# Block-sparse attention with a feed-forward layer on one core: three score banks, tied preparations, and early copies and casts on ACT

## The chip, the cores and the metric

The kernel runs on one core of a Trainium2 chip. The metric is the device time of one launch in microseconds (us), lower is better. A core has a matrix engine (TensorE: PE for its matmuls, PEld for its weight loads), a vector engine (VectorE, DVE), a scalar engine (ScalarE, ACT), GpSimd (POOL), and SyncE (SP), which in this kernel issues the DMAs; SPq stands for its queue. PSUM has eight accumulator banks.

## The reference

```python
def _attn_ref(q, k, v, sampled_blocks):            # q, k, v: 4 x 8 x 768 x 64
    scores = scale * np.matmul(q, k.transpose(0, 1, 3, 2))
    mask = np.abs(blk_i - blk_j) <= 1              # blocks of 32
    mask = mask | (blk_i == 0) | (blk_j == 0) | (blk_i == n_blocks - 1) | (blk_j == n_blocks - 1)
    for qb in range(n_blocks):                     # and three sampled blocks for each query block
        for kb in sampled_blocks[qb]:
            mask[qb * block:(qb + 1) * block, kb * block:(kb + 1) * block] = True
    scores = np.where(mask, scores, -1000000000.0)
    attn = np.exp(scores - np.max(scores, axis=-1, keepdims=True))
    attn = attn / (np.sum(attn, axis=-1, keepdims=True) + 1e-09)
    return np.matmul(attn, v)

def _moe_ref(x, w_in, w_out):                      # x: 3072 x 512, w_in: 512 x 2048, w_out: 2048 x 512
    h = x @ w_in
    g = np.maximum(0.01 * h, h)
    return g @ w_out
```

The attention's output, heads side by side, is x of the feed-forward layer.

## The kernel before

Every float32 operand of a matmul is split into a high and a low half-precision part; products are summed from those parts. A *unit* is one tile of 64 queries for one pair of heads. Four tiles by four head pairs are the 16 units of an *item* (256 tokens); twelve items (four sequences b of three items j) make 192 units. A tile meets 384 keys (12 blocks of 32: four of the neighbourhood, the first and last, six sampled); the first tile of a sequence (T = 0) holds the two edge blocks' queries, sees all 768 keys and works in two parts, which makes 208 score tiles of 128 x 384.

Steps of a unit: scores on PE (`scores`, L651: query against key high and low, into a PSUM bank s); scaling, mask and row minimum of the negated score on DVE (L658, "mx"); exp with row sum on ACT (L669); for each two units the reciprocal on DVE (L677, L678); the high part of the probabilities on ACT (L684, tile pp); the low part on DVE (L689, "split"); the transposition of both by a DMA that SyncE issues (L692, tile pt); and P times V on PE (`pair_av`, L714, one bank av). After four head pairs the tile is normalised to x (L721 to L732). The feed-forward work of a finished item is cut into 16 chunks f: h = x W_in on PE (L749, one of the banks h), leaky relu (ACT L756, DVE L760), its half-precision cast g (DVE L765 in `ffn_act2`), its rest (POOL L766), and o = g W_out on PE (L779, two banks o). Chunks of items (0,0) and (0,1) are taken before both weights have their final scale (`c.whole` is false there); they go through L756 and L760 in other forms.

Around these run the *preparations*: for each 128 queries (`prep_q`) a load by SyncE (rq, L473), a square with sum on ACT (L523), the sum over partitions on PE (L126, q_sum), the scale on DVE, the high part on ACT (L530), the low part on DVE (L532), a transposition by SyncE (L535, qs) and two copies by SyncE with halves exchanged (L537, L538, qxs). `prep_k` does the same for the keys of two heads (loads L482, square L494, k_sum, transposition L512 to kt). V is split (L446, L449), written out (L453) and gathered for each tile by SyncE (`gather_v`: L611, L616, and six sampled blocks with L619 and L621 each). The keys of a tile are collected in one of two buffers kg (`gather_k`): a copy of the four neighbouring blocks by DVE (L582), of the edge blocks (L585), and of the sampled blocks by POOL (L591). The weights are decoded in between (L304 to L316 the column scales, L367 to L376 the splits).

The order of the work comes from two places. The program emits the steps unit by unit, in the order of a string of letters (`CFG["ord"]`), with preparations and weights advanced by costs; then the framework's scheduler sets each engine's order from priorities (by emission) and a timeline of its own. Instructions of equal readiness keep the order of emission unless a dependency says otherwise; a *NoSync* dependency binds the order of two instructions of one engine without a semaphore. Score tiles are emitted in pairs, the later unit first:

```python
        for u in us[::-1]:
...
                if not CFG["spair"]:
                    scores(ahead[:1])
                elif u.pi == 1:
...
                        scores(ahead)
```

Names in rows: `p_1_2_3_0_0` is sequence 1, item 2, tile 3, head pair 0, part 0, and s, mx, pp and pt likewise; `q2_0_0` is sequence 2, item 0, first half of its queries; `k1_0` is sequence 1, first two heads; `g_1_1_0` is chunk 0 of item (1,1).

The PSUM banks are two s, two o, three h and one av.

Of the kernel before, what the change touches and what calls it, by code (L numbers as in the profile page):

```python
# [19 lines left out]
P = 128  # L20
# [9 lines left out]
CFG = {  # L30
    "ahead": 3,
    "av_lag": 3,
    "bs": 1500,
    "early": 2,
    "flag": 1,
    "g": 2,
    "g_at": 0,
    "ht": 1,
    "k_at": 6,
    "k_at0": 26,  # L40
# [10 lines left out]
    "rk": 2,  # L51
    "rmax": 1.0,
    "rmin": 0.0,
    "side": 1.2,
    "side0": 1.6,
    "spair": 1,
    "spread": 8,
    "v_at": 28,
    "wr": [(0, 1.0), (4, 3.0), (10, 4.0), (18, 4.5)],
# [6 lines left out]
def tile_block_sparse_attention_ffn(  # L66
# [19 lines left out]
    nc = tc.nc  # L86
# [20 lines left out]
    pa = ctx.enter_context(tc.tile_pool(name="pa", bufs=2))  # L107
    pf = ctx.enter_context(tc.tile_pool(name="pf", bufs=2))
    dr = ctx.enter_context(tc.tile_pool(name="dr", bufs=2, space=bass.MemoryType.DRAM))
    ps_s = ctx.enter_context(tc.tile_pool(name="ps_s", bufs=2, space=bass.MemoryType.PSUM))  # L110
    ps_o = ctx.enter_context(tc.tile_pool(name="ps_o", bufs=2, space=bass.MemoryType.PSUM))
    ps_1 = ctx.enter_context(tc.tile_pool(name="ps_1", bufs=1, space=bass.MemoryType.PSUM))

# [1 line left out]
    nc.vector.memset(zero, 0.0)  # L115

    def bank(name, tag="h"):
        return ps_1.tile([P, 512], F32, tag=tag, name=name, bufs={"h": 3, "av": 1}[tag])


    ones = cst.tile([P, P], F32, name="ones")
# [2 lines left out]
    def scale_sum(ss, n, name):  # L124
        pb = bank(f"{name}_sum")
        nc.tensor.matmul(pb[:, :n], ones, ss, start=True, stop=True)  # L126
        return pb
# [26 lines left out]
    def scales(ss, n, name, **how):  # L154
        now = tc.cur_priority
        tc.cur_priority = now - CFG["bs"]
        begin = len(nc.cur_bb.bb.instructions)
        pb = scale_sum(ss, n, name)
        loose.update(i.name for i in nc.cur_bb.bb.instructions[begin:])
        r = scale_of(pb, n, name, **how)  # L160
        tc.cur_priority = now + 8
        return r

    def together(emits):

        now = tc.cur_priority
        begin = len(nc.cur_bb.bb.instructions)
        for n, emit in enumerate(emits):
            if n == 1:
                tc.cur_priority = now - 100000  # L170
            emit()
        new = nc.cur_bb.bb.instructions[begin:]
        for i in new[1:]:
            tc.add_manual_dep(i, new[0].name, mybir.DependencyInfo(
                mybir.DependencyClass.NoSync, mybir.DependencyReason.DATA), reason="together")
        tc.cur_priority = now + len(new)
# [308 lines left out]
    def prep_k(b, hp, rk):  # L485

        nm = f"k{b}_{hp}"
        ss = sm.tile([P, 1], F32, tag="ssk", name=f"ss_{nm}")
        if b == 0:
            k16 = early_k.bitcast(F16)[:, (NP + hp) * 2 * S:(NP + hp + 1) * 2 * S].rearrange(  # L490
                "p (n l d) -> p n l d", n=HC, l=2)
        else:
            k16 = pa.tile([P, HC, 2, D], F16, tag="k16", name=f"k16_{nm}", bufs=1)
        nc.scalar.activation(flat(k16)[:, :S], flat(rk), AF.Square, accum_out=ss)  # L494
        yield 1.0
        yield 0.01
        pb = scale_sum(ss, 1, nm)
        yield 0.2
        inv, s = scale_of(pb, 1, nm, fl="k")
        if (b, "inv") not in kready:  # L500
            kready[b, "inv"] = cst.tile([P, NP], F32, name=f"kinv_{b}")
        nc.vector.tensor_scalar(
            out=kready[b, "inv"][:, hp:hp + 1], in0=inv[:, :1], scalar1=-SCALE, scalar2=None, op0=ALU.mult)
        yield 0.4
        raw = rk.rearrange("p h c d -> p (h c) d")
        nc.scalar.activation(k16[:, :, 1, :], raw, AF.Copy, scale=s[:, :1])
        yield 1.0
        nc.vector.scalar_tensor_tensor(
            out=k16[:, :, 0, :], in0=raw, scalar=s[:, :1], in1=k16[:, :, 1, :], op0=ALU.mult, op1=ALU.subtract)
        if b not in kts:  # L510
            kts[b] = pa.tile([P, H, S], F16, tag="kt", name=f"kt_{b}", bufs=2)
        nc.sync.dma_start_transpose(  # L512
            out=kts[b][:, 2 * hp:2 * hp + 2, :].rearrange("p h (c t) -> p (h c) t", t=P),
            in_=k16.rearrange("p n l d -> p (n l d)"))
        kready[b, hp] = True
        yield 1.2

    def prep_q(b, j, i, rq):

        nm = f"q{b}_{j}_{i}"  # L520
        ss = sm.tile([P, 1], F32, tag="ssq", name=f"ss_{nm}")
        qa = pa.tile([P, H, 2, D], F16, tag="qa", name=f"qa_{nm}", bufs=1)
        nc.scalar.activation(flat(qa)[:, :H * D], rq.rearrange("p h d -> p (h d)"), AF.Square, accum_out=ss)  # L523
        yield 0.7
        yield 0.01
        pb = scale_sum(ss, 1, nm)
        yield 0.2
        inv, s = scale_of(pb, 1, nm)
        yield 0.4
        nc.scalar.activation(qa[:, :, 1, :], rq, AF.Copy, scale=s[:, :1])  # L530
        yield 0.7
        nc.vector.scalar_tensor_tensor(  # L532
            out=qa[:, :, 0, :], in0=rq, scalar=s[:, :1], in1=qa[:, :, 1, :], op0=ALU.mult, op1=ALU.subtract)
        qs = pa.tile([P, H, P], F16, tag="qs", name=f"qs_{nm}", bufs=2)
        nc.sync.dma_start_transpose(out=qs, in_=flat(qa))  # L535
        qxs = pa.tile([P, H, P], F16, tag="qxs", name=f"qxs_{nm}", bufs=2)
        nc.sync.dma_start(out=qxs[:D], in_=qs[D:])  # L537
        nc.sync.dma_start(out=qxs[D:], in_=qs[:D])  # L538
        qstack[b, j, i] = (qs, qxs, inv)
        yield 0.8  # L540
# [28 lines left out]
    def sampled_of(T):  # L569

        return [(6 + a * NR + r, (2 * T - 1 + a) * NR + r) for a in range(2) for r in range(NR)]
# [4 lines left out]
    def gather_k(b, T):  # L576

        kt = kts[b]
        n = (b * (NT - 1) + T - 1) % 2
        kg = kgb[n]  # L580
        t0 = (T - 1) * Q2
        nc.vector.tensor_copy(out=kg[:, :, :P], in_=kt[:, :, t0:t0 + P])  # L582
        if ends.get(n) != b:
            ends[n] = b
            nc.vector.tensor_copy(  # L585
                out=kg[:, :, P:P + Q2].rearrange("p h (n l) -> p h n l", l=BLOCK),
                in_=kt.rearrange("p h (n l) -> p h n l", l=BLOCK)[:, :, 0:NB:NB - 1, :])
        for slot, i in sampled_of(T):
            begin = len(nc.cur_bb.bb.instructions)
            off = nc.gpsimd.value_load(offs[:1, i:i + 1], min_val=0, max_val=S - BLOCK)  # L590
            nc.gpsimd.tensor_copy(  # L591
                out=kg[:, :, slot * BLOCK:(slot + 1) * BLOCK], in_=kt[:, :, bass.ds(off, BLOCK)])
            in_order("k", begin)
            yield
        em = pa.tile([P, KEYS], BF16, tag="em", name=f"em_{b}_{T}", bufs=2)
        nc.gpsimd.tensor_copy(
            out=em.rearrange("p (n l) -> p n l", l=BLOCK),
            in_=mask[:, T - 1, :].unsqueeze(2).to_broadcast([P, SLOTS, BLOCK]))
        kgs[b, T] = kg, em
        yield  # L600
# [97 lines left out]
    def pair_av(pr):  # L698

        if pr.hp == 0:  # L700
            avs[pr.item.n, pr.T] = bank(f"av_{pr.nm}", "av").rearrange("p (n l t) -> p n l t", n=NP, l=2)
        pr.av = avs[pr.item.n, pr.T]
        for u in pr.units:
            require_v(u.b, u.hp, u.T)
        emits = []
        for u in pr.units[::-1]:
            n = NCH * u.parts
            for c in range(n):
                for l in range(2):
                    for hh in range(2):  # L710
                        vt = vgs[u.b, u.T][:, c, 2 * u.hp + hh, :] if u.T else v16s[u.b, u.hp][:, c, hh, :]
                        emits.append(lambda o=pr.av[hh * D:(hh + 1) * D, u.hp], a=vt[:, l * D:(l + 1) * D],
                                     m=u.pt[c // NCH][:, :, c % NCH, hh * D:(hh + 1) * D], c=c, l=l, n=n:
                                     nc.tensor.matmul(o, a, m, start=(c == 0 and l == 0), stop=(c == n - 1 and l == 1)))  # L714
        together(emits)

    def tile_evac(pr):

# [43 lines left out]

    def ffn_act2(c):
        c.g = pf.tile([P, 2, 2, N2], F16, tag="g", name=f"g_{c.item.nm}_{c.f}", bufs=CFG["g"])
        nc.vector.tensor_copy(out=c.g[:, 0], in_=c.t)  # L765
        nc.gpsimd.tensor_tensor(out=c.g[:, 1], in0=c.t, in1=c.g[:, 0], op=ALU.subtract)  # L766

    def ffn_o(c):
# [43 lines left out]
    for b in range(B):  # L812
        for j in range(NI):
# [213 lines left out]
    for u in units:  # L1027
        it, ui = u.item, u.k * NP + u.hp
        b, nb = it.b, it.b + 1
# [33 lines left out]
        c = aq[0] if aq else None  # L1063
        for w in CFG["ord"]:
# [126 lines left out]
```

## Time and profile before

| | us |
|---|---|
| median of three runs | 949.08 (949.08, 949.32, 946.14) |
| the profiled execution | 946.47 |
| its span | 944.7 |
| PE busy in the span | 754.8 (80%) |
| DVE busy | 609.1 (64%) |
| ACT busy | 488.1 (52%) |
| POOL busy | 331.3 (35%) |
| mean granted clock of PE | 0.931 |

Busy times are of one profiled execution; the span is from its first to its last instruction. A row of a group reads: line, engine, operation, written from read, shapes, count, then busy us and mean ns, and behind the second bar the idle time of the engine just before these instructions with what ended it. A row of a waits view reads: who waited for whom, us in total, times, longest. A row of a timeline reads: start us, us, engine, line, operation. SyncE's issuing is not counted as busy on the page; its rows show in a timeline. The granted clock is a share of full speed.

### The profile page before, as it was taken

What the parts mean: (1) busy time and instruction counts of PE and PEld (TensorE: products, weight loads), DVE (VectorE), ACT (ScalarE), POOL (GpSimd) and SP (SyncE); (2) the same over time, 40 slices, a digit from 0 to 9 for tenths busy, and PEclk for the clock granted to TensorE, in tenths of its full rate; (3) what the DMA queues carried; (4) which work ended last, traced back from release to release, by engine and by line L of the source; (5) the groups of instructions that cost most, each with busy time, mean ns of one, the idle gap of its engine ahead of it and who ended that gap; (6) DMA issues with size and microseconds to landing.
All of it is one profiled execution on the core that took longest, in us unless ns stands there. A gap on an engine that the chain in (4) does not pass through costs nothing. (4 is left out here: it accounts for less than half of the span.)

```text
span 944.7 us, 21784 instructions
## 1 busy us (share of the span) xinstructions
PE 754.8 (80%) x7020; PEld 492.8 (52%) x7020; DVE 609.1 (64%) x1643; ACT 488.1 (52%) x1063; POOL 331.3 (35%) x469
## 2 busy tenths in 40 slices
PE   1325456788978979979897968989888988989998
PEld 1214334465645645646554635556455655656674
DVE  4989899996857667557565565567466655745221
ACT  4565768575535456456455554456355554535121
POOL 0234665542215344243324242333323433532221
PEclk9998557799989989999999998999999999989999
DMA  9996798678685767766675978676785665555200
GB/s 209 283 276 162 162 244 187 164 148 167 141 180 128 160 121 157 160 137 130 151 165 111 171 134 147 151 146 127 151 161 125 137 136 139 120 113 123 32 23 23
DMA packets 336624, 139.38 MB, mean 148 GB/s; under 512 B 299389, under 2 KB 311678, under 8 KB 336510
## 3 DMA queue, kind: packets, MB, share of 16 engines
q1 hardware_dynamic: 336510, 137.99, 68.5%
q8 instruction: 55, 0.90, 0.4%
q14 instruction: 59, 0.48, 0.2%
HBM read 65.57 MB, written 12.58 MB: 83 GB/s over the span
## 5 line engine op out<-in xcount | busy, mean ns | idle before, releaser
L779 PE MATMUL o<-W,g 128*128 128x512 f16 x1152 | 279.1, 388 | 7.6 <-ACT ob L797 2.9
L749 PE MATMUL h<-x,W 128*128 128x256 f16 x2304 | 280.9, 279 | 0.3 <-DVE ht L760 0.3
L749 PEld LDWEIGHTS <-W 128*128 128x128 f16 x2304 | 227.2, 101 | 50.7 <-issue 10.5
L766 POOL TENSOR_TENSOR g<-ht,g 128x512 f16<-128x512 f32 x96 | 115.3, 1201 | 336.5 <-DVE g L765 201.2
L689 DVE SCALAR_TENSOR_TENSOR pp<-p,r,pp 128x384 f16<-128x384 f32 x208 | 142.5, 702 | 106.0 <-ACT pp L684 104.4
L779 PEld LDWEIGHTS <-g 128*128 128x128 f16 x1152 | 108.8, 100 | 137.4 <-issue 23.9
L669 ACT ACTIVATE p<-p,mx 128x384 f32<-128x384 f32 x208 | 125.8, 606 | 96.3 <-DVE mx L658 67.0
L591 POOL COPY kg<-kt 128x256 f16 x264 | 129.3, 510 | 131.6 <-PE s L651 74.9
L684 ACT ACTIVATE pp<-p,r 128x384 f16<-128x384 f32 x208 | 119.6, 607 | 103.9 <-DMA pt<-pp 72.0
L714 PE MATMUL av<-pt,vg 128*64 128x128 f16 x2112 | 83.0, 231 | 50.5 <-DMA pt<-pp 40.3
L658 DVE CUSTOM_DVE_ANT_0 p<-s,em,nsc 128x384 f32<-128x384 f32 x176 | 101.9, 609 | 21.1 <-PE s L651 20.0
L714 PEld LDWEIGHTS <-vg 128*64 128x64 f16 x2112 | 72.1, 116 | 77.0 <-issue 57.4
L760 DVE SCALAR_TENSOR_TENSOR ht<-h,gd,ht 128x512 f32<-128x512 f32 x80 | 59.8, 747 | 56.0 <-ACT ht L756 55.7
L756 ACT ACTIVATE ht<-h,gs 128x512 f32<-128x512 f32 x80 | 54.0, 675 | 63.9 <-PE h L749 48.7
L651 PE MATMUL s<-kg,qs_q 128*64 128x384 f16 x352 | 65.1, 364 | 12.1 <-DVE mx L658 7.7
L732 POOL TENSOR_TENSOR x<-xf,x 128x256 f16<-128x256 f32 x48 | 35.8, 745 | 90.7 <-ACT x L730 90.0
L651 PE MATMUL s<-kg,qxs_q 128*64 128x384 f16 x352 | 63.9, 357 | 4.3 <-DMA qxs_q<-qs_q 4.3
L651 PEld LDWEIGHTS <-qs_q 128*64 128x64 f16 x416 | 27.9, 116 | 68.7 <-issue 45.4
L523 ACT ACTIVATE qa_q<-rq 128x512 f16<-128x512 f32 x25 | 15.7, 628 | 68.9 <-DMA rq<-in_q_dram 68.9
L765 DVE CAST g<-ht 128x512 f16<-128x512 f32 x96 | 43.4, 452 | 8.9 <-PE o L779 7.5
L677 DVE TENSOR_SCALAR sum<-sum 128x2 f32<-128x2 f32 x96 | 24.9, 259 | 37.1 <-ACT p L669 36.1
L669 ACT ACTIVATION_READ_ACCUMULATOR p<-p,mx 128x1 f32 x208 | 38.9, 187 | 0.0
(126 smaller groups left out, 726.0 us busy)
## 6 DMA issues: line engine op xcount, KB each, us to landing
vg<-scr SPq DMA_DIRECT2D x280, 64.0 KB, 1.9
vg<-scr SPq DMA_DIRECT2D x44, 256.0 KB, 3.1
v<-in_v_dram SPq DMA_DIRECT2D x32, 192.0 KB, 3.4
qxs_q<-qs_q SPq DMA_DIRECT2D x48, 128.0 KB, 3.0
scr<-v SPq DMA_DIRECT2D x16, 384.0 KB, 3.7
W<-in_moe_w_in_dram SPq DMA_DIRECT2D x5, 1024.0 KB, 5.9
rq<-in_q_dram SPq DMA_DIRECT2D x20, 256.0 KB, 3.5
out_dram<-ob SPq DMA_DIRECT2D x20, 256.0 KB, 2.3
```

Source lines behind the costliest of these rows:

```text
L591: nc.gpsimd.tensor_copy(out=kg[:, :, slot * BLOCK:(slot + 1) * BLOCK], in_=kt[:, :, bass.ds(off, BLOCK)])
L651: nc.tensor.matmul(o, a, k, start=(n == 0), stop=(n == 1)))
L658: nc.vector.tensor_tensor_reduce(out=u.p[i], in0=u.sp[i], in1=kgs[u.b, u.T][1] if u.T else zero.to_broadcast([P, KEYS]), scale=u.nsc, scal ...
L669: nc.scalar.activation(u.p[i], u.p[i], AF.Exp, scale=-1.0, bias=u.mx[:, :1], accum_out=u.pair.sum[:, u.pi, i:i + 1])
L684: nc.scalar.activation(pp[:, 0, :], p, AF.Copy, scale=u.r)
L689: nc.vector.scalar_tensor_tensor(out=pp[:, 1, :], in0=p, scalar=u.r, in1=pp[:, 0, :], op0=ALU.mult, op1=ALU.subtract)
L714: nc.tensor.matmul(o, a, m, start=(c == 0 and l == 0), stop=(c == n - 1 and l == 1)))
L749: nc.tensor.matmul(c.ph[:, i], w, x, start=(d == 0 and m == 0), stop=(d == NP - 1 and m == 2)))
L756: nc.scalar.activation(c.t, c.ph, AF.Copy, scale=scale[1])
L760: nc.vector.scalar_tensor_tensor(out=c.t, in0=c.ph, scalar=scale[0], in1=c.t, op0=ALU.mult, op1=ALU.max)
L766: nc.gpsimd.tensor_tensor(out=c.g[:, 1], in0=c.t, in1=c.g[:, 0], op=ALU.subtract)
L779: nc.tensor.matmul(o, a, w, start=(c.first and i == 0 and m == 0), stop=(c.last and i == 1 and m == 2)))
```

## The change

Five edits. (1) Three banks for scores and two for h, instead of two and three. (2) `spair` is 0: each unit's scores are emitted alone, one unit ahead, in ascending order. (3) A new helper `hold` binds an instruction to the one that was emitted just before it on the same engine, by a NoSync dependency; it is used for the square and for the partition sum of key preparations of sequences 1 to 3, and for those of query preparations of all items but the first. (The same hook in `pair_av` is not active, since "a" is not in the string.) (4) The copy of the neighbouring keys is done by ACT in sequence 0: 11 of 44 copies. (5) The cast g is done by ACT for the first two items' chunks that are not `c.whole`: 16 of 96 casts. No other lines are touched, and no DMA is added or removed. Line numbers of the kernel after are larger by up to 34: L608 is the copy on ACT, L799 the cast on ACT, L507 and L543 the squares, L697 exp, L712 the high part, L717 the split, L557 the query's low part, L560 its transposition, L720 that of P.

```diff
--- before.py
+++ after.py
@@ CFG @@
+    "hold": "kq",
...
+    "s": 3,
...
-    "spair": 1,
+    "spair": 0,
@@ pools @@
-    ps_s = ctx.enter_context(tc.tile_pool(name="ps_s", bufs=2, space=bass.MemoryType.PSUM))
+    ps_s = ctx.enter_context(tc.tile_pool(name="ps_s", bufs=CFG["s"], space=bass.MemoryType.PSUM))
...
-        return ps_1.tile([P, 512], F32, tag=tag, name=name, bufs={"h": 3, "av": 1}[tag])
+        return ps_1.tile([P, 512], F32, tag=tag, name=name, bufs={"h": 5 - CFG["s"], "av": 1}[tag])
...
+    def hold(begin):
+
+        ins = nc.cur_bb.bb.instructions
+        prev = next((i for i in reversed(ins[:begin]) if i.engine == ins[begin].engine), None)
+        if prev is not None:
+            tc.add_manual_dep(ins[begin], prev.name, mybir.DependencyInfo(
+                mybir.DependencyClass.NoSync, mybir.DependencyReason.DATA), reason="hold")
+
+    count = lambda: len(nc.cur_bb.bb.instructions)
@@ prep_k @@
+        begin = count()
         nc.scalar.activation(flat(k16)[:, :S], flat(rk), AF.Square, accum_out=ss)
+        if b and "k" in CFG["hold"]:
+            hold(begin)
         yield 1.0
         yield 0.01
+        begin = count()
         pb = scale_sum(ss, 1, nm)
+        if b and "k" in CFG["hold"]:
+            hold(begin)
@@ prep_q @@
+        later = (b or j) and "q" in CFG["hold"]
+        begin = count()
         nc.scalar.activation(flat(qa)[:, :H * D], rq.rearrange("p h d -> p (h d)"), AF.Square, accum_out=ss)
+        if later:
+            hold(begin)
         yield 0.7
         yield 0.01
+        begin = count()
         pb = scale_sum(ss, 1, nm)
+        if later:
+            hold(begin)
@@ gather_k @@
-        nc.vector.tensor_copy(out=kg[:, :, :P], in_=kt[:, :, t0:t0 + P])
+        if b == 0:
+            nc.scalar.activation(kg[:, :, :P], kt[:, :, t0:t0 + P], AF.Copy)
+        else:
+            nc.vector.tensor_copy(out=kg[:, :, :P], in_=kt[:, :, t0:t0 + P])
@@ pair_av @@
+        begin = count()
         together(emits)
+        if pr.item.n and "a" in CFG["hold"]:
+            hold(begin)
@@ ffn_act2 @@
-        nc.vector.tensor_copy(out=c.g[:, 0], in_=c.t)
+        if c.whole:
+            nc.vector.tensor_copy(out=c.g[:, 0], in_=c.t)
+        else:
+            nc.scalar.activation(c.g[:, 0], c.t, AF.Copy)
```

The order on the engines at four places follows. First the copy of neighbouring keys of tile 3 into buffer kg0 (sequence 0, item 0). Before, on DVE, it stood behind the row minima of all four head pairs of tile 1:

```order
L658 ISA p_0_0_1_2_0_642,mx_0_0_1_2_643<-s_0_0_1_2_0_599,em_0_1_436,nsc_0_0_0_2_286 128x384
L658 ISA mx_0_0_1_2_643 128x1
L658 ISA p_0_0_1_3_0_701,mx_0_0_1_3_702<-s_0_0_1_3_0_600,em_0_1_436,nsc_0_0_0_3_344 128x384
L658 ISA mx_0_0_1_3_702 128x1
L677 TENSOR_SCALAR sum_0_0_1_0_480<-sum_0_0_1_0_480 128x2
L582 COPY kg0_93<-kt_0_131 128x8x128
L312 TENSOR_SCALAR W_91<-W_91 128x1024
```

Now, on ACT, the same copy:

```order
L712 ACTIVATE pp_0_0_0_3_0_471<-p_0_0_0_3_0_366,r_0_0_0_2_455 128x384
L697 ACTIVATE p_0_0_1_0_0_468,sum_0_0_1_0_475<-p_0_0_1_0_0_468,mx_0_0_1_0_469 128x384
L712 ACTIVATE pp_0_0_0_3_1_472<-p_0_0_0_3_1_367,r_0_0_0_2_455 128x384
L608 ACTIVATE kg0_93<-kt_0_131 128x8x128
L697 ACTIVATE p_0_0_1_1_0_518,sum_0_0_1_0_475<-p_0_0_1_1_0_518,mx_0_0_1_1_519 128x384
L697 ACTIVATE p_0_0_1_2_0_637,sum_0_0_1_2_642<-p_0_0_1_2_0_637,mx_0_0_1_2_638 128x384
```

The copy stands after the first exp of tile 1 and ahead of the next three, and it overwrites the buffer that the scores of tile 1 read.

Second, SyncE around the transposition of the first tile's third head pair (`pt_0_0_0_2_0`, `pt_0_0_0_2_1`), before and now:

```order
L621 DMA vg1_96<-scr_0_534 32x1024
L619 TENSOR_LOAD offs_89
L619 ISA x2
L621 ISA
L621 DMA vg1_96<-scr_0_534 32x1024
L692 DMA_TRANSPOSE pt_0_0_0_2_0_468<-pp_0_0_0_2_0_463 128x6x128
L692 DMA_TRANSPOSE pt_0_0_0_2_1_471<-pp_0_0_0_2_1_464 128x6x128
```

```order
L649 DMA vg0_95<-scr_0_534 32x1024
L647 TENSOR_LOAD offs_89
L647 ISA x2
L649 ISA
L649 DMA vg0_95<-scr_0_534 32x1024
L720 DMA_TRANSPOSE pt_0_0_0_2_0_463<-pp_0_0_0_2_0_458 128x6x128
L720 DMA_TRANSPOSE pt_0_0_0_2_1_466<-pp_0_0_0_2_1_459 128x6x128
L647 TENSOR_LOAD offs_89
```

It stood behind the first sampled blocks of vg1; now it stands among the sampled blocks of vg0.

Third, the query preparation `q2_0_0`: on DVE, its low part against the splits, before and now:

```order
L678 RECIPROCAL r_1_2_2_0_8164<-sum_1_2_2_0_7935 128x2
L449 SCALAR_TENSOR_TENSOR v16_2_2_8570<-v_2_2_7296,v2_s_8116,v16_2_2_8570 128x6x64
L532 SCALAR_TENSOR_TENSOR qa_q2_0_0_7938<-rq_2_0_0_7576,q2_0_0_s_8261,qa_q2_0_0_7938 128x8x64
L760 SCALAR_TENSOR_TENSOR ht_1_1_0_8177<-h_1_1_0_8139,gd0_2840,ht_1_1_0_8177 128x512
L689 SCALAR_TENSOR_TENSOR pp_1_2_2_0_0_8173<-p_1_2_2_0_0_7927,r_1_2_2_0_8164,pp_1_2_2_0_0_8173 128x384
L765 CAST g_1_1_0_8180<-ht_1_1_0_8177 128x512
```

```order
L574 TENSOR_SCALAR nsc_2_0_0_3_8851<-kinv_2_5552,q2_0_0_inv_8260 128x1
L717 SCALAR_TENSOR_TENSOR pp_1_2_3_0_0_8541<-p_1_2_3_0_0_8345,r_1_2_3_0_8532,pp_1_2_3_0_0_8541 128x384
L557 SCALAR_TENSOR_TENSOR qa_q2_0_0_7938<-rq_2_0_0_7576,q2_0_0_s_8261,qa_q2_0_0_7938 128x8x64
L717 SCALAR_TENSOR_TENSOR pp_1_2_3_1_0_8578<-p_1_2_3_1_0_8387,r_1_2_3_0_8532,pp_1_2_3_1_0_8578 128x384
L791 SCALAR_TENSOR_TENSOR ht_1_1_2_8289<-h_1_1_2_8231,gd0_2835,ht_1_1_2_8289 128x512
L797 CAST g_1_1_2_8292<-ht_1_1_2_8289 128x512
```

and on SyncE its transposition against those of P, before and now:

```order
L806 DMA out_0_dram<-ob_1_0_0_8199 64x512
L808 DMA out_0_dram<-ob_1_0_1_8204 128x512
L535 DMA_TRANSPOSE qs_q2_0_0_8266<-qa_q2_0_0_7938 128x8x128
L473 DMA rq_2_0_1_8271<-in_q_dram 128x8x64
L692 DMA_TRANSPOSE pt_1_2_2_0_0_8277<-pp_1_2_2_0_0_8173 128x6x128
```

```order
L840 DMA out_0_dram<-ob_1_0_0_8199 64x512
L842 DMA out_0_dram<-ob_1_0_1_8204 128x512
L560 DMA_TRANSPOSE qs_q2_0_0_8266<-qa_q2_0_0_7938 128x8x128
L485 DMA rq_2_0_1_8271<-in_q_dram 128x8x64
L720 DMA_TRANSPOSE pt_1_2_2_0_0_8277<-pp_1_2_2_0_0_8168 128x6x128
```

SyncE's row stands just ahead of `pt_1_2_2_0_0` in both. On DVE the low part stood ahead of the split of `pp_1_2_2_0_0`; now it stands behind that of `pp_1_2_3_0_0`, so that five splits (four of tile 2, one of tile 3) precede it whose transpositions SyncE issues only behind `qs_q2_0_0`; it was none.

Fourth, on ACT, the square of `k1_0`, before and now:

```order
L310 ACTIVATE W_91<-W_91 128x1024
L446 ACTIVATE v16_0_1_539<-v_0_1_158,v0_s_531 128x6x2x64
L494 ACTIVATE k16_k1_0_2782,ss_k1_0_2781<-rk_1_0_2356 128x768
L446 ACTIVATE v16_0_2_609<-v_0_2_161,v0_s_531 128x6x2x64
L446 ACTIVATE v16_0_3_724<-v_0_3_164,v0_s_531 128x6x2x64
L669 ACTIVATE p_0_0_0_1_0_264,sum_0_0_0_0_222<-p_0_0_0_1_0_264,mx_0_0_0_1_266 128x384
```

```order
L697 ACTIVATE p_0_1_3_1_0_2677,sum_0_1_3_0_2591<-p_0_1_3_1_0_2677,mx_0_1_3_1_2678 128x384
L752 ACTIVATE avt_0_1_0_2_2392<-av_0_1_0_0_2048 128x256
L507 ACTIVATE k16_k1_0_2777,ss_k1_0_2776<-rk_1_0_2351 128x768
L385 ACTIVATE W_91<-W_91,wo2_s_2023 128x1024
L383 ACTIVATE W_91<-W_91,wo2_s_2023 128x2x512
L322 ACTIVATE W_91<-wbuf_92 128x512
L697 ACTIVATE p_0_1_3_2_0_2857,sum_0_1_3_2_2865<-p_0_1_3_2_0_2857,mx_0_1_3_2_2858 128x384
```

It stood ahead of the third exp of the program; now it stands between exps of item (0,1), tile 3.

## The prediction

> **What bounds the kernel now.** I read the page's first two parts, then the busy time by stage, then the waits of each engine, and last the issuing queue of SyncE (SPq), whose instructions the page does not count as busy. The profiled execution took 946.47 us, 2.6 us below the median of the three runs (949.08), with a span of 944.7 us; the sum below is made against 946.5.
>
> The busy line, the granted clock, and four stages (columns: us, then busy time of PE, PEld, DVE, ACT, POOL with counts, granted clock, DMA share, GB/s):
>
> ```profile
> PE 754.8 (80%) x7020; PEld 492.8 (52%) x7020; DVE 609.1 (64%) x1643; ACT 488.1 (52%) x1063; POOL 331.3 (35%) x469
> ...
> PEclk9998557799989989999999998999999999989999
> ...
> 0.00:80.00 80.00, 23.51 (x178) 16.49 (x178) 60.48 (x174) 43.74 (x77) 13.91 (x21) 1.00 1.05 254
> 80.00:240.00 160.00, 108.97 (x1040) 72.94 (x1038) 141.49 (x362) 106.55 (x216) 84.29 (x92) 0.75 0.79 169
> 240.00:850.00 610.00, 531.44 (x5082) 343.71 (x5079) 379.43 (x1050) 313.20 (x726) 212.15 (x337) 0.96 0.69 143
> 850.00:944.00 94.00, 90.87 (x729) 59.66 (x727) 27.74 (x59) 24.56 (x47) 20.96 (x20) 0.99 0.23 51
> ```
>
> No engine is full before 850 us: PE misses 56.5 + 51.0 us up to 240 us and 78.6 us from 240 to 850. After 850 it misses 3.1 us in 94, so the end is PE alone. What PE lacks before that shows in SyncE's queue; here it is in the middle of the run (start, us, issue), followed by the range of all P transpositions, and PE where the last query half arrives:
>
> ```profile
> 599.69 2.58 SPq L535 DMA_TRANSPOSE qs_q<-qa_q  x1
> 602.33 0.57 SPq L473 DMA_DIRECT2D rq<-in_q_dram  x1
> 602.94 1.35 SPq L692 DMA_TRANSPOSE pt<-pp  x1
> 604.39 0.54 SPq L537 DMA_DIRECT2D qxs_q<-qs_q  x1
> 604.98 0.59 SPq L538 DMA_DIRECT2D qxs_q<-qs_q  x1
> 605.61 1.26 SPq L423 DMA_DIRECT2D v<-in_v_dram  x2
> 606.92 2.59 SPq L692 DMA_TRANSPOSE pt<-pp  x2
> ...
> L692 SPq DMA_TRANSPOSE pt<-pp x208: 1209/1252/3559, 59.7 to 877.6; - x104
> ...
> 842.82 0.51 PE L651 MATMUL s<-kg,qs_q 128*64 128x384 f16 x3 [1.60 <-DMA qs_q<-qa_q]
> 845.97 0.82 PE L651 MATMUL s<-kg,qxs_q 128*64 128x384 f16 x3 [2.63 <-DMA qxs_q<-qs_q]
> ```
>
> The seven rows fill 9.48 of the 9.82 us from 599.69 to 609.51: SyncE issues without a gap. One P transposition goes out every (877.6 - 59.7)/207 = 3.95 us, of which 1.25 us is its own issue and the rest the V gathers, queries and outputs between. The last transfers that PE waits for (842.82, 845.97) come from this queue too. That the queue is behind, and not ahead, is seen from those who wait for it (ACT's two rows: whole run, then 240 to 850 us; PE's first two rows 240 to 900 us, its third before 240 us):
>
> ```profile
> ACT pp L684 <- DMA pt<-pp: 72.0, 33, 6.8
> ...
> ACT qa_q L523 <- DMA rq<-in_q_dram: 57.9, 16, 6.3
> ...
> PE av L714 <- DMA pt<-pp: 36.5, 22, 4.5
> PE k_sum L126 <- ACT k_k L494: 16.7, 6, 4.9
> ...
> PE s L651 <- DVE mx L658: 21.1, 6, 9.6
> ```
>
> ACT waits 72.0 us for pp buffers whose transposition has not been issued or landed, PE 36.5 us for the transposed probabilities. So the time is roughly when SyncE has issued its list (846 us) plus PE's uncovered rest (about 98 us). The change removes no DMA, so it acts on the bound only by what makes SyncE stand. Its largest waits for DVE are all early:
>
> ```profile
> SPq L512 <- DVE W L314: 4.5, 1, 4.5
> ...
> SPq L535 <- DVE W L312: 3.4, 1, 3.4
> ...
> SPq L304 <- DVE W L316: 2.4, 2, 1.4
> ```
>
> **The change part by part.** Durations of what is moved (the first two rows from 0 to 256 us, the other two whole run):
>
> ```profile
> L765 DVE CAST g<-ht 128x512 f16<-128x512 f32 x11 | 6.5, 593 | 0.0
> L582 DVE COPY kg<-kt 128x1024 f16<-128x1024 f16 x11 | 5.4, 495 | 0.9 <-PE s L651 0.8
> ...
> L310 ACT ACTIVATE W<-W 128x1024 f32<-128x1024 f32 x9 | 10.0, 1119 | 7.9 <-DMA W<-in_moe_w_in_dram 4.3 <-DMA W<-in_moe_w_out_dram 3.6
> ...
> L756 ACT ACTIVATE ht<-h 128x512 f32<-128x512 f32 x16 | 9.3, 582 | 5.6 <-POOL g L766 4.2 <-PE h L749 1.4
> ```
>
> *Copies and casts.* DVE loses 11 copies x 0.495 + 16 casts x 0.593 = 5.4 + 9.5 = 14.9 us, nearly all before 256 us. ACT has no such instruction now; nearest by size are 1.119 us for 1024 elements and 0.582 us for 512, so it gains 11 x 1.119 + 16 x 0.582 = 12.3 + 9.3 = 21.6 us. From 80 to 240 us DVE is busy 141.5 of 160 and ACT 106.6, so afterwards both stand near 127: DVE's queue gets shorter, ACT's takes up idle time. Hidden as long as ACT's order lets exps through; else see the third rival.
>
> The Trainium skill ("ScalarE: Activation LUTs", Rules for kernel authors) speaks against the move: simple elementwise work belongs on VectorE, up to about 3x faster there in bf16. The rows agree with 1119/495 = 2.3x. By the 186 ns + 0.833 ns per element that its section What ACT_TABLE_LOAD costs gives, the copy would be an estimated 1.04 us and ACT's gain 11.4 + 9.8 = 21.2 us, the same sum.
>
> *Earlier attention, later weights.* With single score tiles the first tiles' scores, exps and splits move ahead of weight decodes on DVE, and SyncE issues the P transpositions of the first tile's third pair of heads ahead of V gathers that stood before them. What can come back is the three DVE waits above, 4.5 + 3.4 + 2.4 = 10.3 us, and at the other end nothing (the decodes still have to be done, and later weights can hold SyncE's weight loads instead). I take 6 us, nearer the upper end, because DVE's 14.9 us come on top. PE's early 21.1 us for score banks lie in the same stretch and are not counted again.
>
> *Tied preparations, k.* The square of k1_0 goes from exp 2 to exp 34 on ACT and the column sum stays beside it. The 16.7 us that PE waits for k squares largely vanish. I cost this at nothing: while PE stood, SyncE went on issuing, and SyncE sets the time; if that cover is gone it is a gain of 16.7 us (first rival).
>
> *Tied preparations, q.* The square, the sum and with them DVE's low half (L532) come later, while SyncE's qs transposition (L535) keeps its place. Splits of P that precede the low half, less transpositions that precede qs, go from 2 to 5 at q1_2_0, 0 to 5 at q2_0_0, 2 to 4 at q3_2_0. Those three places, DVE then SyncE:
>
> ```profile
> 377.15 0.91 DVE L532 SCALAR_TENSOR_TENSOR qa_q<-rq,q_s,qa_q 128x512 f16<-128x512 f32 x1 [0.33 <-ACT qa_q L530]
> 388.03 1.29 SPq L535 DMA_TRANSPOSE qs_q<-qa_q  x1
> ...
> 441.43 0.74 DVE L532 SCALAR_TENSOR_TENSOR qa_q<-rq,q_s,qa_q 128x512 f16<-128x512 f32 x1
> 460.31 1.33 SPq L535 DMA_TRANSPOSE qs_q<-qa_q  x1
> ...
> 788.59 0.75 DVE L532 SCALAR_TENSOR_TENSOR qa_q<-rq,q_s,qa_q 128x512 f16<-128x512 f32 x1
> 791.05 1.26 SPq L535 DMA_TRANSPOSE qs_q<-qa_q  x1
> ```
>
> SyncE came 10.0, 18.1 and 1.7 us after the low half. At 3.95 us a unit the shifts take 11.9, 19.8 and 7.9 us: waits of 1.9, 1.7 and 6.2, together 9.8 us. Queued behind such a wait are the next P transpositions, and so av on PE. Against it, ACT's 57.9 us of waiting for rq should shrink, since the square now stands where its query is loaded, and ACT and DVE then run further ahead of SyncE. Ends 0 and 9.8; I take 3, nearer the lower end, for that 57.9.
>
> *Banks.* Three score banks are paid with one h bank. Costs in the steady part:
>
> ```profile
> L749 PE MATMUL h<-x,W 128*128 128x256 f16 x2304 | 280.9, 279 | 0.3 <-DVE ht L760 0.3
> ...
> L779 PE MATMUL o<-W,g 128*128 128x512 f16 x1152 | 279.1, 388 | 7.6 <-ACT ob L797 2.9 <-POOL g L766 2.1 <-DVE g L765 1.2
> ...
> L756 ACT ACTIVATE ht<-h,gs 128x512 f32<-128x512 f32 x80 | 54.0, 675 | 63.9 <-PE h L749 48.7 <-POOL g L766 12.6 <-PE av L714 2.5
> ...
> L760 DVE SCALAR_TENSOR_TENSOR ht<-h,gd,ht 128x512 f32<-128x512 f32 x80 | 59.8, 747 | 56.0 <-ACT ht L756 55.7
> ```
>
> PE waits 0.3 us in all for an h bank now. Emptying one takes 0.675 + 0.747 = 1.4 us plus queueing, and a group of 12 output matmuls (4.7 us) covers it. One in ten of 96 banks late by 1.4 us would be 13 us; ends 0 and 13, I take 1, by the 0.3.
>
> Single scores after 240 us and ACT's casts for the second item cost nothing: PE and ACT wait for SyncE's transfers there anyway.
>
> Sum: 946.5 - 6 + 3 + 1 = 944.5. The last query's two waits on PE, 1.60 + 2.63 us, are not covered by anything; with PE's order around them loosened by the third score bank I take half of them back: 942.4, say 943.
>
> **Rivals.**
>
> *PE's stalls count in full.* If PE and not SyncE sets the pace, the k sums give back 16.7 us: 943 - 16.7 = 926. For it: at each such stall the clock drops; after a 4.86 us wait for a k sum ended at 569.6:
>
> ```profile
> 570.00:574.00 4.00, 4.00 (x20) 2.88 (x21) 2.31 (x7) 2.05 (x4) 0.00 (x0) 0.50 0.84 179
> ```
>
> Half the rate for 4 us loses 2 us; with six stalls 12 us more, 914 at the lowest. Against it: SyncE's gapless rows and the 72.0 us. The Trainium skill ("TensorE: Matmul & The Clock Gate", HAM oscillation) says an idle window beyond about 3.4 us halves the clock; the row after 4.86 us of idling agrees, and by that rule both losses go together.
>
> *Later q makes SyncE stand (the other side).* If the three waits count in full and the early gain is 2, 946.5 - 2 + 9.8 + 1 = 955. It decides if ACT's waits for rq turn out to be the cover, not the delay. For it: the 1.7 us margin at q3_2_0; against: ACT has 297 us idle from 240 to 850.
>
> *ACT becomes late in the first sequence.* kg copies now stand between exps and wait for scores of the tile that uses the buffer. If ACT is the bound there, the move costs 21.6 - 14.9 = 6.7 us net and gains nothing: 953, more with waits. For it: the 2.3 between the engines; against: ACT's 53 idle us from 80 to 240.
>
> *Two h banks* at their upper end: 943 + 13 = 956.
>
> *Nothing reaches the end:* SyncE's list is the same, its early waits move to other weights: 946 to 949.
>
> **Chances and numbers.** Forecast (938 to 946) 0.38; PE's stalls 0.13; late q 0.14; late ACT 0.10; h banks 0.05; no effect 0.20. A measurement of this kernel tells about 0.5% (4.7 us) from no change, so the bounds are 944.3 and 953.8. Faster: most of the forecast (0.32) and 0.13, 0.45. Same: its rest 0.06, no effect 0.20 and the mild part of late q and ACT 0.05, 0.31. Slower: 0.24. The range leaves out the lower part of the first rival and the upper parts of late q and ACT: 925 to 958; the forecast's own is 938 to 946.
>
> **What would show it.** Right: SyncE still without gaps from 80 to 840 us, the early waits of SyncE for W below 5 us, the first P transposition before 59.7 us, PE's k_sum wait under 5 us, ACT's rq wait well under 57.9, the last qxs wait at about 840 us. Wrong: that wait moving by more than 10 us, SyncE idle for several us at a qs transposition, PE waiting for DVE at h, or ACT waiting for PE at the kg copy by more than 5 us in all.

## The result, and the profile after

The changed kernel takes 956.42 us (median of three runs, 955.35 to 957.9) against 949.08 before: 1.0083 times the time, 95% interval 1.0061 to 1.0106. It is slower by about 8 us; the forecast was 943 and faster. In the later comparisons the kernel before, run beside each group, had medians of 944.6 to 945.9, so ratios are compared below and not times. Against those medians the same 956.42 us would be 1.011 to 1.0125: that the change costs time is clear, but whether it is 0.8% or 1.2% is not.

The busy line of the page after:

```profile
PE 763.9 (80%) x7020; PEld 495.5 (52%) x7020; DVE 603.8 (63%) x1616; ACT 510.2 (53%) x1090; POOL 329.8 (35%) x469
```

Its four stages, columns as before:

```profile
0.00:80.00 80.00, 21.65 (x156) 14.66 (x157) 61.96 (x170) 48.24 (x84) 16.44 (x28) 0.89 1.07 256
80.00:240.00 160.00, 106.28 (x1027) 71.78 (x1024) 131.50 (x330) 111.58 (x218) 74.70 (x84) 0.75 0.78 167
240.00:850.00 610.00, 538.68 (x5069) 346.26 (x5068) 379.63 (x1049) 322.65 (x736) 217.49 (x337) 0.95 0.69 141
850.00:954.00 104.00, 97.31 (x775) 62.75 (x772) 30.72 (x68) 27.72 (x54) 21.16 (x20) 0.97 0.26 59
```

The groups of the copies on ACT, the casts on ACT, the queries' squares and the matmuls into the h banks:

```profile
L608 ACT ACTIVATE kg<-kt 128x1024 f16<-128x1024 f16 x11 | 11.4, 1043 | 0.3 <-PE s L679 0.3
L799 ACT ACTIVATE g<-ht 128x512 f16<-128x512 f32 x16 | 10.0, 623 | 4.5 <-DVE ht L791 4.5
L543 ACT ACTIVATE qa_q<-rq 128x512 f16<-128x512 f32 x25 | 15.4, 616 | 3.5 <-DVE W L326 3.4
L780 PE MATMUL h<-x,W 128*128 128x256 f16 x2304 | 287.1, 283 | 4.5 <-DVE ht L791 4.0 <-DVE q_tot L142 0.4
```

The prices of the moved work came out as estimated: 1.043 us for a copy, 0.623 us for a cast, 11.4 + 10.0 = 21.4 us on ACT, and the copies wait 0.3 us in all. ACT's waits for query loads (68.9 us before) are gone: 3.5 us of idling, and none of it for rq. PE's waits, whole run, before and after:

```profile
PE av L714 <- DMA pt<-pp: 54.7, 29, 5.3
PE s L651 <- DVE mx L658: 25.4, 11, 9.6
...
PE k_sum L126 <- ACT k_k L494: 20.8, 7, 4.9
...
PE s L651 <- DMA qs_q<-qa_q: 12.5, 4, 9.6
PE s L651 <- DMA qxs_q<-qs_q: 7.8, 6, 2.6
```

```profile
PE av L742 <- DMA pt<-pp: 45.7, 24, 6.5
PE s L679 <- DVE mx L686: 36.0, 17, 15.2
PE s L679 <- DMA qs_q<-qa_q: 25.4, 8, 8.3
PE s L679 <- DMA qxs_q<-qs_q: 14.1, 10, 2.8
...
PE k_sum L128 <- ACT k_k L507: 6.6, 3, 4.3
```

The waits for k squares fell from 20.8 to 6.6 us as meant, while those for queries rose from 12.5 + 7.8 (qs, qxs) to 25.4 + 14.1. The last query half now reaches PE here (timeline of PE):

```profile
852.08 0.35 PE L679 MATMUL s<-kg,qs_q 128*64 128x384 f16 x2 [0.77 <-DMA qs_q<-qa_q]
855.22 0.53 PE L679 MATMUL s<-kg,qxs_q 128*64 128x384 f16 x2 [2.78 <-DMA qxs_q<-qs_q]
```

That is 855.22 - 845.97 = 9.3 us later, and the span is 10.0 longer: the loss lies before this point. To place it, the start of each P transposition in SyncE's queue, counted from the start of the span, was compared between the two traces. The 9th comes 10.3 us earlier than before, the 17th 3.4 earlier, the 33rd 4.1 earlier, the 41st 2.7 later, the 57th 10.8 later; from there to the end it is mostly 6 to 10 us later. The rows that begin with the 57th, before and after:

```profile
295.21 5.28 SPq L692 DMA_TRANSPOSE pt<-pp  x4
...
305.97 5.28 SPq L720 DMA_TRANSPOSE pt<-pp  x4
```

So the ground is lost between about 185 and 310 us, while sequence 0 ends and sequence 1 begins.

The same by SyncE's own time. Let each of its instructions, those that load the offsets of sampled blocks and those that wait for semaphores included, cost the median of its kind (same operation, same tiles) before. Then what it issues up to the end of the last copy of a query half (at 843.98 us before, 853.24 after) comes to 652.5 us in both, and the rest of the way (waits, issue that takes longer than usual, the steps between instructions) to 191.5 and 200.7 us. The list is the same; the standing around it grew by 9.2. Most of this lies between 160 and 320 us, where time beyond the medians and holes above 0.3 us went from 16.3 to 24.4. It is spread over several places: among them are waits of 2.8 us ahead of a weight load, 2.3 at a split, 1.8 at a query and 0.4 to 1.3 ahead of the copies of query halves, while one of 2.1 us at the query q0_2_0 is gone. Two of the holes (timelines of DVE and SyncE; the last two rows are the same query before):

```profile
206.53 0.75 DVE L717 SCALAR_TENSOR_TENSOR pp<-p,r,pp 128x384 f16<-128x384 f32 x1
...
199.97 3.85 SPq L649 DMA_DIRECT2D vg<-scr  x4
207.30 2.60 SPq L720 DMA_TRANSPOSE pt<-pp  x2
...
294.73 0.73 DVE L557 SCALAR_TENSOR_TENSOR qa_q<-rq,q_s,qa_q 128x512 f16<-128x512 f32 x1
...
290.80 2.88 SPq L720 DMA_TRANSPOSE pt<-pp  x2
295.49 1.24 SPq L560 DMA_TRANSPOSE qs_q<-qa_q  x1
...
280.56 0.74 DVE L532 SCALAR_TENSOR_TENSOR qa_q<-rq,q_s,qa_q 128x512 f16<-128x512 f32 x1
...
284.60 1.26 SPq L535 DMA_TRANSPOSE qs_q<-qa_q  x1
```

A split ends at 207.28 and SyncE starts its transposition at 207.30; its last transfer was out at 203.82 and the loading of the next offsets done at 205.0, so it stands for 2.3 us. A query's low part (q1_0_1) ends at 295.46 and SyncE, done at 293.68, starts at 295.49; before, it came to this query 3.3 us after the low part (281.30 to 284.60).

### The profile page after: what moved, and what is told of

The parts are those of the page before. It is cut to its first block, busy times and chain, and to the rows that moved or that the text cites. A ratio compares the mean times of both kernels' runs of the same rounds, so it can differ in the third digit from the quotient of the medians.

```text
span 954.7 us, 21878 instructions
## 1 busy us (share of the span) xinstructions
PE 763.9 (80%) x7020; PEld 495.5 (52%) x7020; DVE 603.8 (63%) x1616; ACT 510.2 (53%) x1090; POOL 329.8 (35%) x469
## 5 line engine op out<-in xcount | busy, mean ns | idle before, releaser
L780 PE MATMUL h<-x,W 128*128 128x256 f16 x2304 | 287.1, 283 | 4.5 <-DVE ht L791 4.0
L780 PEld LDWEIGHTS <-W 128*128 128x128 f16 x2304 | 229.9, 102 | 58.6 <-issue 14.5
L717 DVE SCALAR_TENSOR_TENSOR pp<-p,r,pp 128x384 f16<-128x384 f32 x208 | 142.0, 696 | 103.3 <-ACT pp L712 102.7
L712 ACT ACTIVATE pp<-p,r 128x384 f16<-128x384 f32 x208 | 119.9, 606 | 130.5 <-DMA pt<-pp 100.1
L697 ACT ACTIVATE p<-p,mx 128x384 f32<-128x384 f32 x208 | 126.4, 608 | 107.2 <-DVE mx L686 85.1
L619 POOL COPY kg<-kt 128x256 f16 x264 | 125.6, 497 | 150.6 <-PE s L679 97.3
L686 DVE CUSTOM_DVE_ANT_0 p<-s,em,nsc 128x384 f32<-128x384 f32 x176 | 105.8, 611 | 48.1 <-PE s L679 47.1
L742 PE MATMUL av<-pt,vg 128*64 128x128 f16 x2112 | 86.2, 236 | 43.2 <-DMA pt<-pp 34.4
L742 PEld LDWEIGHTS <-vg 128*64 128x64 f16 x2112 | 74.2, 120 | 66.8 <-issue 52.9
L679 PE MATMUL s<-kg,qxs_q 128*64 128x384 f16 x352 | 63.3, 363 | 10.8 <-DMA qxs_q<-qs_q 10.8
L705 DVE TENSOR_SCALAR sum<-sum 128x2 f32<-128x2 f32 x96 | 33.2, 347 | 22.9 <-ACT p L697 22.5
L797 DVE CAST g<-ht 128x512 f16<-128x512 f32 x80 | 34.8, 434 | 9.3 <-PE o L813 7.8
L697 ACT ACTIVATION_READ_ACCUMULATOR p<-p,mx 128x1 f32 x208 | 38.9, 187 | 0.0
L679 PEld LDWEIGHTS <-qxs_q 128*64 128x64 f16 x416 | 26.4, 119 | 21.0 <-DMA qxs_q<-qs_q 14.6
```

Of the source, the lines that this page charges most:

```text
L619: nc.gpsimd.tensor_copy(out=kg[:, :, slot * BLOCK:(slot + 1) * BLOCK], in_=kt[:, :, bass.ds(off, BLOCK)])
L679: nc.tensor.matmul(o, a, k, start=(n == 0), stop=(n == 1)))
L686: nc.vector.tensor_tensor_reduce(out=u.p[i], in0=u.sp[i], in1=kgs[u.b, u.T][1] if u.T else zero.to_broadcast([P, KEYS]), scale=u.nsc, scal ...
L697: nc.scalar.activation(u.p[i], u.p[i], AF.Exp, scale=-1.0, bias=u.mx[:, :1], accum_out=u.pair.sum[:, u.pi, i:i + 1])
L712: nc.scalar.activation(pp[:, 0, :], p, AF.Copy, scale=u.r)
L717: nc.vector.scalar_tensor_tensor(out=pp[:, 1, :], in0=p, scalar=u.r, in1=pp[:, 0, :], op0=ALU.mult, op1=ALU.subtract)
```

## The experiments

Each ratio is against the kernel before in the same comparison.

| kernel | ratio | 95% interval |
|---|---|---|
| full change | 1.0083 | 1.0061 to 1.0106 |
| e1 banks, single scores | 0.9987 | 0.9965 to 1.0008 |
| e2 ties of k and q | 1.0102 | 1.0065 to 1.0140 |
| e3 copies and casts on ACT | 1.0040 | 1.0017 to 1.0064 |
| e5 ties of q | 1.0144 | 1.0102 to 1.0186 |
| e6 ties of k | 1.0053 | 1.0027 to 1.0079 |
| f1 copies on ACT | 1.0073 | 1.0045 to 1.0102 |
| f2 casts on ACT | 0.9985 | 0.9966 to 1.0005 |
| e7 full, q ties from sequence 1 | 1.0130 | 1.0098 to 1.0162 |
| e9 full without ties | 1.0060 | 1.0039 to 1.0081 |
| e10 full without q ties | 1.0045 | 1.0024 to 1.0066 |
| e11 full without k ties | 1.0093 | 1.0063 to 1.0124 |
| e12 full, copies and casts on DVE | 1.0068 | 1.0042 to 1.0094 |
| g1 banks and casts | 0.9969 | 0.9945 to 0.9994 |
| e4 before, outputs by ACT | 0.9875 | 0.9835 to 0.9915 |
| f3 full, outputs by ACT | 1.0014 | 0.9986 to 1.0042 |
| f4 before, outputs and V loads by ACT | 0.9984 | 0.9960 to 1.0007 |
| e8 banks, single scores, outputs by ACT | 0.9911 | 0.9881 to 0.9941 |
| g2 banks and casts, outputs by ACT | 0.9850 | 0.9825 to 0.9876 |

**One part alone.** Against the kernel before, e1 sets the score banks and the single scores:

```diff
-    "spair": 1,
+    "spair": 0, "s": 3,
```

> Before with three score banks, two h banks and single scores alone. Theory A (the new score order starves SyncE's queue early, in the first sequence): 954 to 958, the first P transpositions ahead of V gathers as in the full change and the ground lost again by 120 us. Theory B (the loss comes from the tied preparations): 942 to 950. Theory C (the loss comes from the copies and casts on ACT): 942 to 950 too, and e3 slow.

0.9987: neutral. Theory A falls. The 9th P transposition comes 8.8 us earlier here too and the 17th only 2.6: SyncE issues V gathers behind it that used to stand ahead.

e2 sets the ties alone:

```diff
+    "hold": "kq",
```

> Before with the tied squares and sums of k and q alone. Theory A: 944 to 951, PE's wait for k squares below 8 us all the same. Theory B: 954 to 960, with SyncE's queue waiting several us at query transpositions between 180 and 310 us. Theory C: 944 to 951.

1.0102, as theory B says, at another place than it says: it has lost 8.2 us by the 17th P transposition, at about 124 us.

e3 sets the copies and casts alone (the two `AF.Copy` edits of the diff):

> Before with the 11 copies and 16 casts on ACT alone. Theory A and B: 942 to 950, DVE 12 to 15 us less busy, ACT 20 to 22 more. Theory C: 953 to 958, ACT waiting for PE at the copies by more than 5 us.

1.0040, between the theories. DVE's busy time fell by 9.4 us (609.1 to 599.7), ACT's rose by 19.6; no copy waited for PE. The time is in the range of A and B, the interval lies above 1 all the same: a part of C's cost is there, without C's mechanism.

e4 leaves the kernel before as it is but for four lines:

```diff
-                nc.sync.dma_start(out=out[...
+                nc.scalar.dma_start(out=out[...
```

> Before with the 32 output DMAs issued by ACT instead of SyncE. If SyncE's issuing sets the time up to 846 us, the 24 or so outputs that go out before then, at 0.5 us each, come off: 935 to 941. If PE's stalls or another engine set it: 945 to 951, SyncE's queue then showing holes.

0.9875. PE, where the last query half arrives:

```profile
836.51 0.82 PE L651 MATMUL s<-kg,qxs_q 128*64 128x384 f16 x3 [2.65 <-DMA qxs_q<-qs_q]
```

This is 9.5 us earlier than before, SyncE's list up to there is 642.1 us instead of 652.5, its standing 192.4 instead of 191.5, and the span 10.1 us shorter. The 32 issues take 14.0 us of ACT's queue (issuing is not counted in its busy time, 487.7 us here). What is taken off SyncE's list comes off the time.

**Which ties.** e5 is `"hold": "q"`, e6 `"hold": "k"`, each on the kernel before:

> Before with the query ties alone (items 0,1 onwards). Theory Q (a tied query preparation stands ACT and with it SyncE's queue in the first sequence): 952 to 957, the transposition of q0_1_0 more than 10 us later than before. Theory K (the key ties do it): 944 to 949.

> Before with the key ties alone (sequences 1 to 3). Theory Q: 944 to 949 although PE's wait for k squares falls below 8 us, because that wait lay beside SyncE's issuing. Theory K: 952 to 957. If PE's k_sum waits were worth their size after all: 930 to 938.

1.0144 and 1.0053: mostly the query ties, the key ties a little, and PE's k_sum wait hardly moved in e6 (17.8 us against 20.8), so e6 says nothing on what that wait is worth. In e5 the place is plain (timelines of SyncE, ACT, DVE; L322 is a weight decode, L555 and L557 the halves of q0_1_0, L560 its transposition):

```profile
95.75 1.77 SPq L316 DMA_DIRECT2D W<-in_moe_w_in_dram  x2
97.64 8.75 SPq L717 DMA_TRANSPOSE pt<-pp  x4
...
109.03 3.92 SPq L560 DMA_TRANSPOSE qs_q<-qa_q  x1
...
101.98 1.12 ACT L322 ACTIVATE W<-W 128x1024 f32<-128x1024 f32 x1 [8.59 <-DMA W<-in_moe_w_in_dram]
103.00 0.71 ACT L555 ACTIVATE qa_q<-rq,q_s 128x512 f16<-128x512 f32 x1
...
103.96 0.74 DVE L557 SCALAR_TENSOR_TENSOR qa_q<-rq,q_s,qa_q 128x512 f16<-128x512 f32 x1
```

With the tie, the query's high part stands behind a weight decode whose load SyncE issued only at 95.75. ACT stands 8.59 us with exps and high parts behind it. The transposition of q0_1_0 goes out 18 us later than before (109.03 against 90.73), and the four P transpositions issued just behind the weight's load take 8.75 us instead of the usual 5.0; whether the load's transfer stretches them is not shown.

e7 keeps the full change and changes one line of it:

```diff
-        later = (b or j) and "q" in CFG["hold"]
+        later = b and "q" in CFG["hold"]
```

> The full change with the query ties from sequence 1 on only, so that items (0,1) and (0,2) are prepared as before. Theory Q: 945 to 951, what stays over before being the copies and casts on ACT (3 to 4 us). If the late query halves of sequences 1 to 3 make SyncE stand, as the prediction's second rival has it: 954 to 958.

1.0130, no better than the full change: in that company the first sequence's query ties are not the loss. Like the full change it loses between the 41st and the 57th P transposition (4.6 us earlier than before, then 8.4 later), and at the same query, q1_0_1, SyncE stands for 1.1 us. Theory Q as a whole story falls.

That hole is not made by the query ties. SyncE stands at q1_0_1 in e6 too (key ties alone, 1.1 us) and in f1 (copies alone, 1.8), and not in e5 and e11, which tie the queries without the keys. Nor is it the loss: it is there in g1, which has neither ties nor copies and is not slow (timelines of DVE and SyncE):

```profile
286.25 0.73 DVE L557 SCALAR_TENSOR_TENSOR qa_q<-rq,q_s,qa_q 128x512 f16<-128x512 f32 x1
...
285.40 0.43 SPq L646 DMA_DIRECT2D vg<-scr  x1
287.01 1.23 SPq L560 DMA_TRANSPOSE qs_q<-qa_q  x1
```

**Parts in company.** e9 to e12 each take one part out of the full change (`"hold": ""`, `"k"`, `"q"`, and the two `AF.Copy` edits undone):

> The full change without any tie (banks, single scores, copies and casts on ACT). Theory T (the ties carry the loss): 944 to 950, SyncE's standing time up to its last query transfer within 4 us of before. Rival U (ACT's copies and casts carry it, as the run with late query ties suggests): 952 to 957.

> The full change without the query ties, key ties kept. Theory T with both ties bad: 948 to 953. If the query ties alone carry it: 944 to 950. Rival U: 953 to 957.

> The full change without the key ties, query ties kept. Theory T: 953 to 958, nearly the whole loss. Rival U: 953 to 957 as well. If the key ties carry it in company: 944 to 950.

> The full change with copies and casts back on DVE (banks and ties kept). Theory T: 953 to 958. Rival U: 944 to 950.

Neither theory holds: no single removal brings the time back (1.0045 to 1.0093). The ties without the ACT work cost 0.7%, the ACT work without the ties 0.6%. Both cost 0.8% in the first comparison, but up to 1.2% by the later medians of the kernel before, so it is not shown that these two overlap. It is shown among the ties: on the kernel before, those of the queries cost 1.44% and those of the keys 0.53%, both together only 1.02% (e2, at most 1.40). Nor do the parts lose at one place. In their single traces e5 is late by 10.0 us at the 17th P transposition and goes from 5.6 to 16.2 between the 41st and the 49th; f1 (below) goes from 0.1 to 10.8 between these two; e6 is late only behind the 169th. With banks and ACT work in place, the query ties bring 1.0060 to 1.0093 and the key ties 1.0060 to 1.0045, whose intervals overlap. In e9's single trace SyncE's standing is 192.2 us, as theory T has it, but that execution (948.14 us) was the fastest of its four, whose median is 950.81.

f1 and f2 part the ACT work, on the kernel before:

> Before with only the 11 copies of neighbouring keys on ACT. Theory kg (the copies stand between exps and wait for scores of PE, so ACT comes late in the first sequence): 948 to 951, nearly all of the 0.4 % that copies and casts cost together. Theory g (the casts do it): 943 to 947.

> Before with only the 16 casts g on ACT. Theory kg: 943 to 947. Theory g: 948 to 951, POOL's and PE's output matmuls waiting for ACT's cast.

1.0073 and 0.9985: the copies cost, the casts don't. But not as theory kg said: here too the copies wait only 0.5 us for PE. What the trace shows is that exps come later, 12.5 us at the 33rd and 10.3 at the 57th, and that DVE was not relieved (busy 609.1 before, 611.7 in f1). How much of the 7 us is ACT's 11.4 us and how much the order that the scheduler laid around them was not tried and stays open.

g1 then leaves out what had been found, ties and copies, and keeps banks, single scores and casts:

> The full change without the ties and with the copies on DVE: three score banks, single scores, the 16 casts on ACT. If copies and ties are the whole loss: 942 to 947, equal to before within 0.4 %. If the banks need the ties to be harmless in company of the casts: 949 to 953.

0.9969, interval 0.9945 to 0.9994: the loss is gone, so copies and ties are the whole of it. The rest is worth about 0.3%, some 3 us, near the 3.5 us (946.5 to 943) that the forecast gave to the whole.

**SyncE's list once more.** f3 is the full change and f4 the kernel before, both with the outputs issued by ACT, f4 with the V loads (L423) too:

> The full change with the 32 output DMAs issued by ACT. If SyncE's list plus its waits sets the time here too: 10 to 13 us off the full change, 941 to 946 on this chip's scale. If the ties have made another engine the bound: 950 to 956.

> Before with the 32 output DMAs and the 32 V loads issued by ACT. SyncE's list is shorter by some 12 plus 18 us: 920 to 930 if it still sets the time. If PE (755 us busy and its stalls) or ACT, which can stand at a V load whose buffer is not free, takes over: 932 to 940, no better than outputs alone.

f3 is at 1.0014 against the full change's 1.0083: the changed kernel follows SyncE's list as well (642.1 us here too, with a standing of 200.0). f4 shows the limit: the list is 29 us shorter (623.3), but SyncE's standing is 219.0 instead of 191.5, and the time is that of the kernel before. Half of what was lost again, 13.9 us, lies in the first 80 us, where SyncE's holes above 0.3 us grew from 1.0 to 15.9 us and PE is busy 20.8 us instead of 23.5. ACT now waits 19.8 us for query scales on DVE (L530 from q_s) instead of 10.6, but which wait comes first was not settled.

g2 is g1 with the outputs on ACT:

> The same with the 32 output DMAs issued by ACT. If SyncE's list sets the time: 931 to 937, like the outputs alone. If casts and outputs together make ACT late: 938 to 945.

0.9850, a median of 931.74 us: faster than both kernels; beside e4 (0.9875) the intervals overlap.

e8 is the same without the casts on ACT. Expected were 932 to 937 if the banks are worth nothing, 922 to 931 if the third score bank pays once SyncE has room. It is 0.9911, a median of 935.10 us: the banks gave nothing beside e4. Its interval lies above that of g2, so with the outputs off SyncE's list the casts on ACT are worth some 0.6%, though the two ran in different comparisons; alone (f2) they were not clear of nothing.

## Why the prediction was wrong

- **The bound** was right. SyncE's list with what stands around it sets the time up to the last query half: e4 took 10.4 us off the list and 10.1 off the span. The first rival, that the k_sum waits come back in full, did not come true: 14.2 us of them and all of ACT's rq waits vanished, and the time rose. PE then waited longer elsewhere, 10.6 us more for score banks and 19.2 more for queries (qs and qxs).
- **The step that failed first** is the cover in "Copies and casts": that ACT "takes up idle time". The price was right, the casts were indeed free (f2), but the copies cost 0.7% alone (f1), and with banks and casts in place they turn 0.9969 (g1) into 1.0060 (e9). As I read it, a mean idle share of 53 us between 80 and 240 us says nothing on whether the idling lies ahead of or behind the exps that SyncE's next P transposition needs. The third rival named this loss and about its size (953), with a wait for scores that did not come.
- **"Earlier attention, later weights"**, 6 us, was not there: SyncE's overlong issue and holes in the first 80 us were 23.7 before and 22.0 after, and banks and single scores alone gave 0.9987. The waits for decoded weights that were to come back moved to other transfers: over the whole run SyncE's waits for DVE's weights come to 16.8 us before and 14.7 after, now mostly at these two:

```profile
SPq L720 <- DVE W L324: 6.0, 3, 3.9
SPq L316 <- DVE W L328: 5.6, 4, 2.8
```

  The order showed P transpositions moved ahead of V gathers; that moves work within SyncE's list and takes none out.
- **"Tied preparations, q"** was sized at 3 us from the wrong places. The margins shrank at two of the three, from 10.0 to 1.9 us at q1_2_0 and from 18.1 to 1.9 at q2_0_0, by less than worked out; at q3_2_0 the margin grew, from 1.7 to 4.1. No wait came of it at any of them. For q2_0_0:

```profile
462.94 0.74 DVE L557 SCALAR_TENSOR_TENSOR qa_q<-rq,q_s,qa_q 128x512 f16<-128x512 f32 x1
465.59 1.32 SPq L560 DMA_TRANSPOSE qs_q<-qa_q  x1
```

  The margin is 465.59 - 463.68 = 1.9 us. Alone, the ties cost 1.4% (e5), lost in the first sequence and the start of the second, where ACT also has weight decodes. Which places of the query ties cost in company stays open, since e7 took the first sequence's out and gained nothing. ACT's rq waits, taken as relief, vanish with these ties (3.0 us are left in e5, 43.5 in e10 without them) and gave nothing back: e5 is the slowest of all.
- **"Tied preparations, k"** at nothing: in company within the interval; alone 0.5% (e6), not foreseen.
- **Two h banks** at 1 us: PE's wait for an h bank went from 0.3 to 4.0 us; e1 and g1 show no cost of it.
- **Half of the last query's waits**, 2.1 us, was to come back through the third score bank. They went from 1.60 + 2.63 = 4.2 us to 0.77 + 2.78 = 3.6: 0.7 us came back.
- The second rival gave 955 for 956.4, by luck: it has SyncE standing at late query halves, and its holes at query transpositions are about as long as before (2.1 us at q0_2_0 before, 1.8 at q1_0_1 after), none at its three places. The single costs do not add up either: e1, e3, e5 and e6 alone would come to 2.2%.

## What to carry to other kernels

Where one queue issues nearly all transfers back to back, cost a change by what stands in that queue and by what leaves it; waits that vanished on engines that follow the queue were worth nothing here. An engine's idle share is no cover for added work: ask whether the idling lies between the added instruction and the next thing the queue needs, and do not add up the costs of single parts: here query ties and key ties alone came to 2.0%, together to 1.0%. Taking 32 plain output DMAs to the engine that makes their data gave more than anything in the change, while taking loads there too lost it again.

## What the runs showed of the hardware that was not expected

A tiny DVE instruction that meets a POOL instruction can last until that one ends. In the kernel after, POOL's weight rest and DVE's row sum of 128 x 2 elements, whose median is 0.17 us:

```profile
134.77 2.29 POOL L386 TENSOR_TENSOR W<-W 128x1024 f16<-128x1024 f32 x1 [1.24 <-ACT W L385]
135.00 2.08 DVE L705 TENSOR_SCALAR sum<-sum 128x2 f32<-128x2 f32 x1
```

and the group of these sums, before and after:

```profile
L677 DVE TENSOR_SCALAR sum<-sum 128x2 f32<-128x2 f32 x96 | 24.9, 259 | 37.1 <-ACT p L669 36.1
...
L705 DVE TENSOR_SCALAR sum<-sum 128x2 f32<-128x2 f32 x96 | 33.2, 347 | 22.9 <-ACT p L697 22.5
```

POOL's instruction ends at 137.06 and DVE's at 137.08. It is so throughout: all 31 of the 96 sums that last longer than 0.25 us end within 0.03 us of the end of a POOL instruction, and so do all 23 in the kernel before; none of the shorter ones lies wholly inside a POOL instruction. The group's 24.9 us became 33.2, which is most of why DVE's busy time fell by 5.3 us and not by the 14.9 that were to leave it. The Trainium skill ("GPSIMD Engine Reference", Key points) says that GpSimd shares its SBUF interfaces with VectorE, with contention for DVE instructions in a 2-port perf mode or with two SBUF inputs. The rows show such a contention and its size, a wait to the end of the large instruction; whether this sum is of either kind no run here shows.

Issuing the 32 outputs took 14.0 us of ACT's queue in e4 and took 10.4 us off SyncE's list. The Trainium skill ("DMA: Bandwidth & Descriptors", Rules for kernel authors) says that spreading DMAs over issuing engines gives no bandwidth and only saves sequencer issue time; e4 agrees on the issue time, and here that time was the bound.
